# Two DMA queues for loads and stores, and value heads that swap halves as whole rows

## The chip, the cores and the metric

The kernel runs on one core of a Trainium2 chip. The metric is the device time of one execution in microseconds; here four runs gave 533.87 to 536.05 us, with a median of 534.9. The profile is that of one execution, of 533.87 us, in which the core's instructions span 531.9 us.

## The reference

Two layers of the same pair of blocks work on a sequence of 2048 tokens with 512 features, 32 heads of 16. All four blocks read a layer norm of x and add their result to x:

```
for layer in range(2):            # the same weights both times
    x = x + A(layernorm(x))
    x = x + B(layernorm(x))

A: q, k, v = x @ wq, x @ wk, x @ wv, in 4 segments of 512 tokens
   in a segment:  p = softmax(scale * q k^T + mask)    causal, in the segment alone
                  a_dot = p v ; a_mem = phi(q) M / (phi(q) z + 1e-6)
                  o = g * a_mem + (1 - g) * a_dot      g = sigmoid(beta), one per head
   then           M += phi(k)^T v ; z += sum phi(k)
   result         o @ wo

B: q, k, v from x @ wqkv; q, k times w_phi per head
   phi(u) = [softmax(u), softmax(-u)]
   kv = phi(k)^T v and z = sum phi(k), over all tokens
   o = phi(q) kv / (phi(q) z + 1e-6), result o @ wo
```

## The kernel before, in words

x stays in on-chip memory as 16 tiles of 128 tokens (`X`). Each tile is normalised on VectorE (`ln`), with the root taken on GpSimd or ScalarE, and transposed, mostly by a transposing DMA of SyncE (`tr`, L664), so that features stand on partitions. `a_proj` makes keys, queries and values of a segment, `a_att` the attention of a token tile in it, `b_keys` the sums of block B over a segment, and `b_query` its result. `out_proj` transposes the heads' output, multiplies it by the output weights and adds it to x; in the last layer it stores the tile (L1204).

TensorE runs with its array cut in halves of 64 rows: two matmuls, one on partitions 0 to 63 and one on 64 to 127, work side by side (`proj`, `mm`, all recorded at L640). For the products of probabilities and values, half of the heads need their values on the other half of the partitions. So `a_proj` keeps the values of a segment twice: `VT` (pool `pV`), 32 heads with a 17th column of ones, and `VU` (pool `pU`), 16 of the heads with the two partition halves exchanged by two DMAs (L1060, issued at L668). In `VT` heads come in fours, of which the first two are the swapped ones, so each of those DMAs gathers pieces of 2 x 17 values, 68 bytes.

The weights are loaded in `setup`: first four x tiles and the A key and query weights, then (held until tile 3 is normalised) the A value and output weights and x tiles 4 to 7, then (held until tile 7 is normalised) x tiles 8 to 15, the three B weights (`WBraw`) and the B output weights in eight pieces (`WB_o`). All but two small ones are issued by SyncE, at L768. The A value weights are multiplied in place by 1 - g (L855, "gate"). `fold_weights` multiplies w_phi into the B key and query weights: eight transposing DMAs (pX<-pX), eight groups of matmuls (p,pX) and evictions.

The order of all this isn't written out. `Graph` holds every operation with its dependencies, its possible engines and a planned duration. `forward` places operations engine by engine in time by priority, `backward` makes priorities from a placement, and a list of seeds in `STEPS` shifts priorities of some operations at the end; the result is a fixed order for each engine, and waits are put where `emit` finds that they are needed. An operation that may run on one of several engines (an eviction on ScalarE or VectorE, a key mask on VectorE or GpSimd) goes where it can first be placed. The planner keeps one time, `dfree`, at which the loads already issued will have landed. Its durations decide the order alone; the chip decides the times. Where TensorE would stand idle in the plan, it adds matmuls without use (`fill`, L991)[...].

Of the kernel before, what the change touches and what calls it, by code (L numbers as in the profile page):

```python
# [16 lines left out]
H = 32  # L17
# [85 lines left out]
class Graph:  # L103
# [143 lines left out]
    def forward(self, prio, pools, rule):  # L247
# [32 lines left out]
        dfree = 0.0  # L280
# [52 lines left out]
        while len(order) < n + fillers:  # L333
# [25 lines left out]
            for e in TURNS[port_last]:  # L359
# [68 lines left out]
                if o.kb:  # L428
                    dfree = max(dfree, o.end + 1000.0) + o.kb / 0.2
                    o.lat = dfree + 400.0 - o.end  # L430
                order.append(o)
                lt = o.lat if o.lat is not None else LAT[e]
                if o.kind == "d" and e == "sp" and not o.kb:
                    lt = max(lt, dfree - o.end + lt)
# [170 lines left out]
class Kernel:  # L605
# [61 lines left out]
    def dma(self, pairs, n, reads, writes, opens=(), eng="sp", lat=1600.0, label=""):  # L667
        return self.g.op({eng: (650.0 * n, lambda e: [e.dma_start(o, i) for o, i in pairs()])},  # L668
                         reads, writes, opens, kind="d", lat=lat, label=label, ndma=n)
# [91 lines left out]
    def setup(self):  # L761
# [4 lines left out]
        def load(pairs, kb, writes, eng="sp", opens=(), n=1):  # L766
            dur = 780.0 if eng == "pool" else 560.0 if n == 1 else 640.0
            o = self.g.op({eng: (dur * n, lambda e: [e.dma_start(o, i) for o, i in pairs()])}, [], writes, opens, kind="d",  # L768
                          lat=3700.0 if eng == "pool" else 1300.0 + kb / 0.25, label="load", ndma=n, kb=0 if eng == "pool" else kb)
            self.loads.append(o)  # L770
            return o

        def ldx(t0, n):
            load(lambda: [(self.X[:, t0:t0 + n, :], xv[t0 * 128:(t0 + n) * 128, :].rearrange("(t p) d -> p t d", p=128))],
                 128 * n, [R("X", t) for t in range(t0, t0 + n)])

        def ldw(dst, src, res):
            load(lambda: [(dst()[:], src.rearrange("(dt p) o -> p dt o", p=128))], 512, [res])
# [5 lines left out]
        for h in range(2):  # L784
            for k in ("k", "q"):
# [6 lines left out]
        ldw(lambda: self.WA["v"], inp["A_wv"], R("WA", "v"))  # L792
        ldx(4, 4)
        load(lambda: [(self.WA["o"][gi * 64:gi * 64 + 64, 2 * hp:2 * hp + 2, :],
                       inp["A_wo"].rearrange("(hp gi b r) o -> hp gi r b o", hp=2, gi=2, b=2)[hp, gi]) for hp in range(2) for gi in range(2)],
             512, [R("WA", "o")], n=4)
        self.second = len(self.loads)
        ldx(8, 4)
        ldw(lambda: self.WBraw["k"].t, wqkv[:, 512:1024], self.WBraw["k"])
        ldw(lambda: self.WBraw["v"].t, wqkv[:, 1024:1536], self.WBraw["v"])  # L800
        ldx(12, 4)
        ldw(lambda: self.WBraw["q"].t, wqkv[:, 0:512], self.WBraw["q"])
        for g in range(NG):
            load(lambda g=g: [(self.WB["o"][(g % 2) * 64:(g % 2) * 64 + 64, b * 2 + g // 2, :],
                               inp["B_wo"][g * 128 + b * 64:g * 128 + b * 64 + 64, :].rearrange("(h d) o -> d h o", d=16)) for b in range(2)],
                 128, [R("WBo", g)], n=2)
# [47 lines left out]
        for dt in range(4):  # L854
            fn = lambda e, dt=dt: e.tensor_tensor(self.WA["v"][:, dt, :].rearrange("p (h d) -> p h d", h=H),  # L855
                                                  self.WA["v"][:, dt, :].rearrange("p (h d) -> p h d", h=H),
                                                  gt[:, 2, :, None].to_broadcast([128, H, DH]), ALU.mult)
            self.g.op({"dve": (602.0, fn), "pool": (1100.0, fn)}, [R("gt2"), R("WA", "v")], [R("WAv", dt)], label="gate")
# [144 lines left out]
    def a_proj(self, L, s):  # L1003
# [51 lines left out]
        for tp in range(2):  # L1055
            ps = self.T(self.pD, "gen")
            self.vproj(ps, self.WA["v"], [R("WAv", i) for i in range(4)], (2 * tp, 2 * tp + 1), xT, opens=[VT], label="V")
            self.evac(lambda tp=tp: VT.t[:, 2 * tp:2 * tp + 2, :, 0:16], lambda ps=ps: ps.t[:].rearrange("p (t h d) -> p t h d", t=2, h=H),
                      1024, [ps], [VT[2 * tp], VT[2 * tp + 1]], label="Vev")
            self.dma(lambda tp=tp: [(VU.t[64 - 64 * h:128 - 64 * h, 2 * tp:2 * tp + 2].rearrange("p t (u r) c -> p t u (r c)", r=2),  # L1060
                                     VT.t[64 * h:64 * h + 64, 2 * tp:2 * tp + 2].rearrange("p t (u k r) c -> p t u k (r c)", k=2, r=2)[:, :, :, 0])
                                    for h in range(2)], 2, [VT[2 * tp], VT[2 * tp + 1]], [VU[2 * tp], VU[2 * tp + 1]], label="Vx", lat=4000.0)
        if s < 3:
            ps = self.T(self.pD, "gen")

            def phases(ps=ps):
                def item(b, h, g, tt, ph):
                    G = 2 * b + g
                    return (ps.t[:, 512 * b + g * 136:512 * b + g * 136 + 136],
                            st["PhK"][b].t[64 * h:64 * h + 64, g * 512 + tt * 128:g * 512 + tt * 128 + 128],  # L1070
                            VT.t[64 * h:64 * h + 64, tt, 8 * G:8 * G + 8, :], ph == 0 and g == 0 and tt == 0, ph == 1 and g == 1 and tt == 3)
# [41 lines left out]
    def a_att(self, L, s, i):  # L1113
# [9 lines left out]
        for hp in range(2):  # L1123
# [12 lines left out]
            def phases(PV=PV, PTs=PTs, hp=hp, pvv=pvv):  # L1136
# [9 lines left out]
                def item(b, h, gg, hl, j, ph):  # L1146
# [9 lines left out]
                    else:  # L1156
                        val = half(VT.t, h)[:, j, 16 * hp + 8 * gg + 4 * b + hl, :]
# [17 lines left out]
    def out_proj(self, L, t, o, ores, W, wres, store=False, res_pe=False, pe=False, pair=None):  # L1175
# [26 lines left out]
        if store:  # L1202
            self.dma(lambda: [(self.out[0][t * 128:(t + 1) * 128, :], self.X[:, t, :])], 1, [R("X", t)], [], lat=1900.0, label="store")
# [209 lines left out]
def basep(ap):  # L1413
# [17 lines left out]
    830000016, 830000026, 830000031, 830000047, 830000154, 830000166, 830000187, 830000200, 830000233, 830000279,  # L1431
    830000404, 830000410, 830000433, 830000479, 830000580, 830000599, 830000611, 830000784, 830000896, 830000919,
    830001010, 830001382, 830001415, 830001452, 830001504, 830001517, 830002105, 830002116, 830002294, 830002609,
    830002795, 830003279, 830003310, 830003395, 830003781, 830004112, 830004126, 830004203, 830004577, 830004793,
    830004991, 830005011, 830005023, 830005426, 830005440, 830005537, 830005586, 830005719, 830005808, 830006395,
    830006537, 830006565, 830006693, 830006726, 830007056, 830007401, 830007597, 830008013, 830008377, 830008745,
    830008955, 830009116, 830009167, 830009459, 830009499, 830009795, 830010341, 830010604, 830010886, 830010951,
    830011019, 830011698, 830013928, 830014025, 830016905, 830017241, 830017964, 830018111, 830018529, 830018586,
    830021285, 830021587, 830021673, 830023952, 830024198, 830024902, 830026119, 830026354, 830028031, 830029804,
# [53 lines left out]
```

## Time and profile before

| | us |
|---|---|
| median of four runs | 534.9 (533.87 to 536.05) |
| profiled execution | 533.87 |
| its span | 531.9 |
| TensorE busy | 476.4 (90%) |
| ScalarE busy | 449.7 (85%) |
| VectorE busy | 422.1 (79%) |
| GpSimd busy | 139.3 (26%) |
| DMA packets of the main queue | 122288, 32.40 MB, 34.1% of 16 engines' span |
| swaps of values, L668 pU<-pV | 32 issues, 68.0 KB each, 3.0 us to landing at the median |
| transposing DMAs, L664 | 138 issues |
| stores, L668 out_dram<-X | 16 issues, 128.0 KB each, 1.9 us to landing at the median |

An engine is written PE (TensorE), PEld (its weight loads, which overlap the matmuls), DVE (VectorE), ACT (ScalarE), POOL (GpSimd) and SPq (the DMA queue of SyncE). "D<-pQ,pK" means that a tile of pool D is written from tiles of pools pQ and pK; pX holds transposed inputs and raw weights, p is short for the pools p1 and p2. A row of waits gives the microseconds in total, how often, and the longest. Busy shares are averages over stages with different limits, so the stages are looked at one by one. The profile's span begins with the first instruction and ends with the last; the run's time has about 2 us more.

### The profile page before, as it was taken

To read this page: it belongs to the slowest core of one execution; us is meant where nothing else is said; L and a number is where in the kernel's file an instruction comes from. 1 tells how busy PE (TensorE), PEld (TensorE's weight loads), DVE (VectorE), ACT (ScalarE), POOL (GpSimd) and SP (SyncE) were. 2 spreads that over 40 slices of the span, in tenths; PEclk is the share of its full clock that TensorE was granted. 3 is DMA by queue.
4 is the path that set the end of the run, shared out by engine and by line. 5 is a ranking of instruction groups with operands and counts; after the bars stand their busy time and mean duration, and the time that the engine had idled before them with its cause. 6 is when DMAs were issued, how large, how long until landed. Compare 5 with 4: busy or idle time off the path is not lost.

```text
span 531.9 us, 26384 instructions
## 1 busy us (share of the span) xinstructions
PE 476.4 (90%) x12178; PEld 322.2 (61%) x12178; DVE 422.1 (79%) x841; ACT 449.7 (85%) x558; POOL 139.3 (26%) x177
## 2 busy tenths in 40 slices
PE   7988579899999999998999989988999988999887
PEld 3445355566766676765756556565667575655575
DVE  6979278899987888876998868888778986867692
ACT  3889379999889899878798979988989989957894
POOL 5929231440052010000245147521152000100000
PEclk9999799999999999999999989999999999999999
DMA  7176444536224012000147645435112132100265
GB/s 200 45 160 160 99 82 111 64 38 88 43 42 65 14 39 38 14 2 2 25 82 101 102 73 73 92 52 73 42 34 46 49 37 33 23 12 1 52 107 146
DMA packets 122462, 34.10 MB, mean 64 GB/s; under 512 B 109520, under 2 KB 122352, under 8 KB 122352
## 3 DMA queue, kind: packets, MB, share of 16 engines
q1 hardware_dynamic: 122288, 32.40, 34.1%
q8 instruction: 95, 1.56, 1.2%
q14 instruction: 15, 0.12, 0.1%
q0 software_dynamic: 64, 0.02, 0.1%
HBM read 6.32 MB, written 2.10 MB: 16 GB/s over the span
## 4 chain that ended last, share of the span: by engine, by line
PE 48%; ACT 22%; DVE 15%; DMA 8%; issue 3%; SPq 3%; POOL 0%
PE D L640 48%; ACT p L651 14%; DMA p<-p 6%; ACT pP L651 4%; DVE p L1168 2%; SPq L664 2%; DVE stats L913 2%; DVE p L660 1%; DMA pX<-p 1%; DVE pS L1246 1%; ACT p L659 1%; DVE pV L660 1%; DVE pT L1266 1%; DVE p L1341 1%; SPq L1049 1%
## 5 line engine op out<-in xcount | busy, mean ns | idle before, releaser
L651 ACT ACTIVATE p<-D 128x1024 bf16<-128x1024 f32 (+1 forms) x292 | 284.0, 1020 | 44.9 <-PE D L640 42.2
L640 PE MATMUL D<-pQ,pK 64*128 64x256 bf16 (+1 forms) x1344 | 118.3, 261 | 7.2 <-ACT p L651 3.3
L651 ACT ACTIVATE pP<-D 128x768 bf16<-128x768 f32 x128 | 101.8, 820 | 10.9 <-PE D L640 10.1
L921 POOL TENSOR_SCALAR rstd<-mv 128x1 f32<-128x1 f32 x60 | 17.2, 293 | 296.3 <-DVE mv L914 295.4
L1023 POOL TENSOR_SCALAR pK<-p,MK 128x1024 bf16<-128x1024 bf16 x26 | 76.3, 2941 | 34.4 <-DVE p L660 24.4
L640 PEld LDWEIGHTS D<-pQ,pK 64*128 64x128 bf16 x1344 | 56.6, 94 | 43.2 <-ACT p L651 8.8
L640 PE MATMUL D<-pV,p 64*128 64x34 bf16 (+1 forms) x1728 | 67.1, 180 | 1.7 <-issue 1.4
L640 PE MATMUL D<-pU,p 64*128 64x34 bf16 x1536 | 59.8, 176 | 2.2 <-ACT pP L651 0.8
L640 PE MATMUL D<-pU,pP 64*128 64x34 bf16 x1024 | 49.9, 175 | 2.6 <-issue 2.0
L640 PE MATMUL D<-WA_o,p 64*128 64x256 bf16 x520 | 41.4, 280 | 11.9 <-DMA p<-p 10.1
L640 PEld LDWEIGHTS D<-pV,p 64*128 64x128 bf16 x1728 | 50.1, 93 | 2.8 <-issue 2.0
L640 PEld LDWEIGHTS D<-pU,p 64*128 64x128 bf16 x1536 | 46.3, 93 | 7.3 <-ACT pP L651 1.3
L640 PE MATMUL D<-pV,pP 64*128 64x34 bf16 x1024 | 49.9, 175 | 0.3 <-issue 0.3
L1168 DVE TENSOR_TENSOR p<-D,pS 128x256 bf16<-128x256 f32 x112 | 47.1, 421 | 2.8
L913 DVE BATCH_NORM_STATS2 stats<-X 128x6 f32<-128x512 bf16 x64 | 43.4, 686 | 4.0 <-DMA X<-in_A_x_dram 3.2
L1246 DVE TENSOR_REDUCE pS<-p 128x64 f32<-128x1024 bf16 (+1 forms) x36 | 39.0, 1092 | 8.4 <-ACT p L651 8.4
L640 PE MATMUL D<-WB_o,p 64*128 64x256 bf16 x514 | 38.1, 270 | 5.5 <-DMA p<-p 4.1
L1266 DVE TENSOR_TENSOR pT<-D,pT 128x1024 bf16<-128x1024 f32 x32 | 38.8, 1217 | 3.8 <-PE D L640 3.4
L640 PE MATMUL D<-WB_k,pX 64*128 64x512 bf16 (+1 forms) x288 | 33.8, 353 | 6.9 <-issue 4.2
L697 DVE RECIPROCAL pS<-D 128x32 f32<-128x32 f32 (+1 forms) x64 | 20.9, 327 | 20.8 <-PE D L640 20.5
L923 POOL TENSOR_TENSOR rstd<-rstd,mhalf 128x1 f32<-128x1 f32 x60 | 35.5, 597 | 3.5
L1201 DVE TENSOR_TENSOR X<-X,D 128x512 bf16<-128x512 bf16 x32 | 21.8, 681 | 18.3 <-PE D L640 17.9
(124 smaller groups left out, 939.4 us busy)
## 6 DMA issues: line engine op xcount, KB each, us to landing
pQ<-p SPq DMA_DIRECT2D x28, 128.0 KB, 2.2
pU<-pV SPq DMA_DIRECT2D x32, 68.0 KB, 3.0
out_dram<-X SPq DMA_DIRECT2D x16, 128.0 KB, 1.9
X<-in_A_x_dram SPq DMA_DIRECT2D x3, 512.0 KB, 7.1
pX<-in_B_wqkv_dram SPq DMA_DIRECT2D x3, 512.0 KB, 4.9
p<-p SPq DMA_TRANSPOSE x76, 2.7
pX<-p SPq DMA_TRANSPOSE x54, 3.0
X<-in_A_x_dram SPq DMA_DIRECT2D x4, 128.0 KB, 2.5
```

What stands on the lines that cost most here:

```text
L640: ins = e.matmul(out_ap, lhsT, rhs, start=st, stop=sp, tile_position=(basep(lhsT), 0))
L651: return self.g.op({"act": (dur, lambda e: e.activation(out_ap(), in_ap(), func, scale=scale))}, reads, writes, opens, label=label)
L660: "dve": ((340 if fast else n / 0.96 + 65), lambda e: e.tensor_copy(out_ap(), in_ap()))}
L697: return e.reciprocal(o, i)
L913: v(lambda e: e.bn_stats(self.stats[:, t, :], self.X[:, t, :]), 602, [R("X", t)], [R("st", t)], label="bn")
L921: v(lambda e: e.tensor_scalar(rs, self.mv[:, t, 1:2], LN_EPS, None, op0=ALU.add), 240, [R("mv", t)], [R("rstd", t)], eng="pool", label="rstd")
L923: v(lambda e: e.tensor_tensor(rs, rs, self.mhalf[:], ALU.pow), 560, [R("rstd", t), R("mhalf")], [R("rstd", t)], eng="pool", label="rstd")
L1023: return e.tensor_scalar(dst, KT.t[:].rearrange("p (t x c) -> p t x c", x=2, c=64), self.MK[:, 0 if raw else 1, m:m + 1], None, op0=ALU.mult)
L1168: v(lambda e, pvv=pvv, rden=rden, part=part, dst=dst, k=k: e.tensor_tensor(part(dst), pvv()[:, :, k, :, 0:16], rden()[:, :, k, :, None].to ...
L1201: self.v(lambda e: e.tensor_tensor(xt(), xt(), res(), ALU.add), 602, [R("X", t), ps], [R("X", t)], label="res")
L1246: fn = lambda e, sgn=sgn, ev=ev, Z=Z, nz=nz: e.tensor_reduce(Z.t[:, sgn * nz:(sgn + 1) * nz], ev().rearrange("p (h d) -> p h d", d=16), AX ...
L1266: v(lambda e, Vt=Vt, src=src, vt=vt: e.tensor_tensor(vt(Vt, 0, 16), src(), vt(Vt, 16, 17).to_broadcast([128, 2, 2, 2, 16, 8]), ALU.mult), ...
```

## The change

It has three parts, and a new list of seeds.

Loads and stores may be issued by SyncE or by GpSimd: an operation whose engine is "any" has both as candidates, with a planned 560 to 640 ns on one and 780 on the other, and the planner takes whichever can be placed first. That holds for the A value and output weights, x tiles 4 to 15, the B weights and the stores of tiles 0 to 13. The planner's `dfree` becomes one time for each queue.

The A value weights go to a staging tile (`wvraw`, in pool pK) and are multiplied by 1 - g from there into `WA["v"]`, with the heads permuted: the two swapped heads of each four come first, 16 in a row, then the 16 others. The four in-place operations become eight of half the width.

So in `VT` the swapped heads are its first 16, and each swap DMA moves a row of 16 x 17 values, 544 bytes, per partition and tile. The matmuls that read `VT` follow: the memory update takes its eight heads from two places and writes its result in the old order, the probability product counts its heads otherwise. The planner's time for a swap goes from 4000 to 2500 ns.

```diff
-        dfree = 0.0
+        dfree = dict.fromkeys(ENGS, 0.0)
...
-                    dfree = max(dfree, o.end + 1000.0) + o.kb / 0.2
-                    o.lat = dfree + 400.0 - o.end
+                    dfree[e] = max(dfree[e], o.end + (1000.0 if e == "sp" else 2000.0)) + o.kb / 0.2
+                    o.lat = dfree[e] + 400.0 - o.end
...
-    def dma(self, pairs, n, reads, writes, opens=(), eng="sp", lat=1600.0, label=""):
-        return self.g.op({eng: (650.0 * n, lambda e: [e.dma_start(o, i) for o, i in pairs()])},
+    def dma(self, pairs, n, reads, writes, eng="sp", opens=(), lat=1600.0, label=""):
+        return self.g.op({k: ((650.0 if k == "sp" else 780.0) * n, lambda e: [e.dma_start(o, i) for o, i in pairs()]) for k in ((eng,) if eng != "any" else ("sp", "pool"))},
...
         def load(pairs, kb, writes, eng="sp", opens=(), n=1):
-            dur = 780.0 if eng == "pool" else 560.0 if n == 1 else 640.0
-            o = self.g.op({eng: (dur * n, lambda e: [e.dma_start(o, i) for o, i in pairs()])}, [], writes, opens, kind="d",
+            dur = {"pool": 780.0 * n, "sp": (560.0 if n == 1 else 640.0) * n}
+            o = self.g.op({k: (dur[k], lambda e: [e.dma_start(o, i) for o, i in pairs()]) for k in ((eng,) if eng != "any" else dur)}, [], writes, opens, kind="d",
...
         def ldw(dst, src, res):
-            load(lambda: [(dst()[:], src.rearrange("(dt p) o -> p dt o", p=128))], 512, [res])
+            load(lambda: [(dst()[:], src.rearrange("(dt p) o -> p dt o", p=128))], 512, [res], "any")
...
-        ldw(lambda: self.WA["v"], inp["A_wv"], R("WA", "v"))
-        ldx(4, 4)
+        self.wvraw = self.T(self.pK, "raw")
+        wvr = lambda: self.wvraw.t[:].rearrange("p (t o) -> p t o", t=4)
+        ldw(wvr, inp["A_wv"], self.wvraw)
+        ldx(4, 4, "any")
...
         for dt in range(4):
-            fn = lambda e, dt=dt: e.tensor_tensor(self.WA["v"][:, dt, :].rearrange("p (h d) -> p h d", h=H),
-                                                  self.WA["v"][:, dt, :].rearrange("p (h d) -> p h d", h=H),
-                                                  gt[:, 2, :, None].to_broadcast([128, H, DH]), ALU.mult)
-            self.g.op({"dve": (602.0, fn), "pool": (1100.0, fn)}, [R("gt2"), R("WA", "v")], [R("WAv", dt)], label="gate")
+            for w in range(2):
+                def fn(e, dt=dt, w=w):
+                    src = wvr()[:, dt, :].rearrange("p (u w r d) -> p w u r d", w=2, r=2, d=DH)[:, w]
+                    one = gt[:, 2, :].rearrange("p (u w r) -> p w u r", w=2, r=2)[:, w]
+                    dst = self.WA["v"][:, dt, 256 * w:256 * w + 256].rearrange("p (u r d) -> p u r d", r=2, d=DH)
+                    return e.tensor_tensor(dst, src, one[:, :, :, None].to_broadcast([128, 8, 2, DH]), ALU.mult)
+                self.g.op({"dve": (340.0, fn), "pool": (700.0, fn)}, [R("gt2"), self.wvraw], [R("WAv", (dt, w))], label="gate")
...
-            self.dma(lambda tp=tp: [(VU.t[64 - 64 * h:128 - 64 * h, 2 * tp:2 * tp + 2].rearrange("p t (u r) c -> p t u (r c)", r=2),
-                                     VT.t[64 * h:64 * h + 64, 2 * tp:2 * tp + 2].rearrange("p t (u k r) c -> p t u k (r c)", k=2, r=2)[:, :, :, 0])
-                                    for h in range(2)], 2, [VT[2 * tp], VT[2 * tp + 1]], [VU[2 * tp], VU[2 * tp + 1]], label="Vx", lat=4000.0)
+            self.dma(lambda tp=tp: [(VU.t[64 - 64 * h:128 - 64 * h, 2 * tp:2 * tp + 2], VT.t[64 * h:64 * h + 64, 2 * tp:2 * tp + 2, 0:H // 2])
+                                    for h in range(2)], 2, [VT[2 * tp], VT[2 * tp + 1]], [VU[2 * tp], VU[2 * tp + 1]], label="Vx", lat=2500.0)
...
-                            VT.t[64 * h:64 * h + 64, tt, 8 * G:8 * G + 8, :], ph == 0 and g == 0 and tt == 0, ph == 1 and g == 1 and tt == 3)
+                            VT.t[64 * h:64 * h + 64, tt].rearrange("p (w x) c -> p w x c", w=2)[:, :, 4 * G:4 * G + 4, :]
+                            .rearrange("p w (u r) c -> p w u (r c)", u=2), ph == 0 and g == 0 and tt == 0, ph == 1 and g == 1 and tt == 3)
...
-                        val = half(VT.t, h)[:, j, 16 * hp + 8 * gg + 4 * b + hl, :]
+                        val = half(VT.t, h)[:, j, 16 + 8 * hp + 4 * gg + 2 * b + hl - 2, :]
...
-            self.dma(lambda: [(self.out[0][t * 128:(t + 1) * 128, :], self.X[:, t, :])], 1, [R("X", t)], [], lat=1900.0, label="store")
+            self.dma(lambda: [(self.out[0][t * 128:(t + 1) * 128, :], self.X[:, t, :])], 1, [R("X", t)], [], "any" if t < 14 else "sp", lat=2200.0, label="store")
...
-STEPS = (210 seeds, 830000016 to 830141651)
+STEPS = (162 seeds, 910000047 to 910145185)
```

In the new order GpSimd issues the A value weights, the three B weights, one of the two later groups of four x tiles, half of the pieces of `WB_o` and 12 of the 16 stores.

## The prediction

> **What bounds the kernel now.** I read the slices of the span first, then the busy time by stretch, the waits of TensorE, and last the DMA queue of SyncE.
>
> The slices (each digit a tenth, 13.3 us wide):
>
> ```profile
> PE   7988579899999999998999989988999988999887
> ACT  3889379999889899878798979988989989957894
> PEclk9999799999999999999999989999999999999999
> ```
>
> TensorE is at 9 nearly everywhere; it is the bound, with ScalarE close behind. The hole is in slices 5 and 6, where the granted clock dips too. The stretches round it (columns: busy us of TensorE, its weight loads, VectorE, ScalarE, GpSimd; clock; DMA share; GB/s):
>
> ```profile
> 40.00:50.00 10.00, 8.80 (x296) 5.94 (x292) 9.86 (x23) 10.00 (x13) 9.58 (x11) 1.00 0.72 179
> 50.00:60.00 10.00, 5.56 (x118) 4.16 (x112) 5.37 (x14) 6.04 (x7) 6.53 (x8) 0.83 0.47 95
> 60.00:70.00 10.00, 7.01 (x172) 4.95 (x172) 3.97 (x11) 4.47 (x6) 2.58 (x6) 0.83 0.48 93
> 70.00:80.00 10.00, 6.78 (x214) 5.05 (x216) 7.80 (x18) 7.54 (x10) 3.00 (x4) 1.00 0.45 85
> 80.00:90.00 10.00, 9.27 (x230) 6.13 (x228) 8.70 (x17) 9.53 (x11) 1.84 (x2) 1.00 0.46 113
> ```
>
> From 50 to 80 us TensorE is idle 30 - 19.35 = 10.65 us. From 80 to 160 it is idle 5.75 us, 0.72 per 10 us, so 8.5 us are extra. At clock 0.83 the 12.6 us of matmul in 50 to 70 also cost about 2.1 us more. ScalarE is idle 11.95 us there and VectorE 12.86: all starve together, so no other engine eats up what is won here. What TensorE waits for in 50 to 82:
>
> ```profile
> PE D L640 <- DMA p<-p: 4.3, 2, 4.0
> PE D L640 <- DMA pX<-pX: 2.7, 1, 2.7
> PE D L640 <- DMA pX<-p: 1.6, 1, 1.6
> ```
>
> All are transposes issued by SyncE; pX<-pX are the eight that the folding of the B weights needs. Why they are late, in the timeline of SyncE's queue (start, us, line, what):
>
> ```profile
> 34.19 1.13 SPq L768 DMA_DIRECT2D pX<-in_B_wqkv_dram  x2
> 35.36 1.06 SPq L768 DMA_DIRECT2D X<-in_A_x_dram  x2
> 36.46 0.51 SPq L768 DMA_DIRECT2D pX<-in_B_wqkv_dram  x1
> 37.02 5.31 SPq L668 DMA_DIRECT2D pU<-pV  x2
> 42.37 6.59 SPq L768 DMA_DIRECT2D WB_o<-in_B_wo_dram  x6
> ...
> 51.09 3.83 SPq L664 DMA_TRANSPOSE pX<-pX  x2
> ...
> 60.24 1.27 SPq L664 DMA_TRANSPOSE p<-p  x1
> ...
> 70.53 1.28 SPq L664 DMA_TRANSPOSE pX<-pX  x1
> ```
>
> Five loads of 512 KB go out at once, and the small transfers behind them stand still: 5.31 us for two swaps and 6.59 for six loads of 64 KB, where a median issue takes 0.67 and 0.59 us. The queue never rests from 34 to 74 us, so the folding starts at 51.1 and its last transpose leaves at 70.5.
>
> **What the skill says.** "DMA: Bandwidth & Descriptors", Issuing engines are not separate DMA queues: all issuers share 16 DMA engines, and a second one saves issue time alone. Same page, Queues, rings and completion order: each DMA engine goes round-robin between the rows it has work for, packet by packet. So a second issuer brings no bandwidth, but a small transfer no longer stands behind megabytes. The trace of before agrees with the first half: with one queue 37 to 42 us moved 363 GB/s while two swaps took 5.31 us. No run yet shows the round robin. "SBUF — State Buffer", SBUF: two separate sides: DMAs of GpSimd have their descriptors written by software, which VectorE's two-port operations can lock out. Before has only two such DMAs, so this is untested:
>
> ```profile
> L768 POOL DMA_DIRECT2D wphi_st<-in_B_w_phi_dram x1 | 0.8, 797 | 0.0
> L768 POOL DMA_DIRECT2D beta_sb<-in_A_beta_dram x1 | 0.8, 787 | 0.0
> ```
>
> wphi has 512 pieces and beta 128, at nearly the same issue time; a 512 KB load has 512 pieces too, so I take 0.8 us each.
>
> **The change, step by step.** The order of the built kernel shows what its planner made of the freedom. On GpSimd now: the A value weights, the three B weights, one of the two later groups of four x tiles, half of WB_o and 12 of the 16 stores. On SyncE stay two x loads, WA_o, half of WB_o, 4 stores.
>
> (1) *Load stretch, -7.5 us.* From SyncE's queue between 34 and 71.8 us fall four loads (2.7 to 0.5 us), half of WB_o (7.8 with the waits, to 4 x 0.59 = 2.4), and the jam of the two swaps (5.3 to 1.3): 2.2 + 5.4 + 4.0 = 11.6 us, so the last folding transpose is issued at about 60. It may not start too soon: the loads still wait for the normalised tile 7, which now stands in VectorE's order behind some 3.4 us more work (three softplus-type operations 1.5, a mask 0.45, two evictions 1.46): 31.75 + 3.4 = 35.1 instead of 34.2. 2.5 MB at the 363 GB/s measured take 7 us, so the first weight to be folded is in at about 43 and the transposes start there rather than at 51. TensorE's own queue: counting matmul pairs at 0.215 us (512 columns), 0.109 (256) and 0.026 (34), all from spacings in the trace, before has 39.9 us of work ahead of the first fold and 51.2 ahead of the first B projection, reached at 55.6 and 77.9: 11.3 us of work in 22.3. At the pace of the rest (386 us of work in 451, 1.17) it would take 13.2; 9.1 are lost, in keeping with the 10.6 above. I take 9.5. In the new order the folds stand at 35.7 to 47.8 us of work; at a lag of 13 us (15.7 less the 2.7 waited at the first fold) plus 2 the last is reached at about 63, just when its transpose, issued at 60, lands (3.6 us at the median). That is tight, so I leave 2 us lost. Bounds: 0 to -10.6.
>
> (2) *Stores, -1 us.* From 497 us SyncE's queue is full, with nine stores (some 0.58 us each, 5.2 in all) between the last transposes, and TensorE waits 3.8 us for p<-p after 495. GpSimd is idle there (0.00 busy from 480). But the last transposes of the chain left 0.04 us after VectorE had their operand, so little of it was the queue's. Bounds 0 to -3.
>
> (3) *Swap in 544-byte rows, -0.5 us.* A swap falls from 64 x 16 = 1024 pieces of 68 B to 128. Its issue stays near 0.65 us. The two in 425 to 429 took all DMA engines for 2 x (0.56 + 0.45) = 2.0 us, so 32 take some 32 us of the 181 (34.1% of the span) that the queue's packets fill. No wait of TensorE on pU shows, so the gain is only that transposes beside them land sooner. Bounds 0 to -2.
>
> (4) *Gates, +0.3 us.* Four operations of 0.67 us (one 1.52) become eight of half the size, at 0.35 to 0.42 (a 128x256 product with PSUM takes 0.42): 3.0 to 3.4 against 2.7. VectorE is 9.97 of 10 us busy in 20 to 30, so it counts. Bounds 0 to +1.
>
> (5) *Issues on GpSimd, +0.5 us.* Nine before 45 us, 9 x 0.79 = 7.1 us, fall into its idle time (29.3 to 39.0) and 3 us beyond; behind them wait the key masks of segment 1 and the roots for tiles 8 to 11. The 12 stores have nothing behind them. Bounds 0 to +2, and rival B.
>
> (6) *Free.* The memory-update matmuls read 2 x 68 columns in two strips, still 136; the values sit elsewhere in V, with no operation added. If strips cost 10%, 96 pairs at 0.06 us make 0.6.
>
> (7) *All orders after 80 us are new.* Work is the same: about 439 us of queued matmuls in both, 561 ScalarE instructions against 560, 166 fillers against 156. I see no sign, so 0, with +-4.
>
> Sum: -7.5 - 1 - 0.5 + 0.3 + 0.5 = -8.2 on the profiled execution's 533.9, 525.7 (span 523.7). The median of the runs is 1.0 above that execution, so 526.7.
>
> **Rivals.** *A, the stretch is hidden or refilled (530 to 536).* The weights come, but TensorE then stands before the next late thing (layer norm, transposes of the B input; pX<-p is already 1.6 us of the waits). For it: slices 5 to 6 hold several kinds of wait. Against: all engines starve together, and 8 transposes leave 11 us earlier. Half of (1): -4 instead of -8.2, 531; nothing: 534.9.
> *B, slower (537 to 546): the software queue delivers the weights late.* Three loads of 512 KB, starved or issued at 2 to 3 us each, push folding behind 51. That is the point from which it decides: weights in at 51 cancel (1), at 60 they cost 9 us: 534.9 + 8 = 543. For it: no large load on GpSimd is in the trace, and VectorE is full there. Against: 0.79 us whatever the piece count; wphi landed in 4.9 us.
> *C, more (516 to 523):* all of (1), -10.6, with stores and swaps at half their bounds, -2.5: 521.8.
>
> **Chances.** Main case (523 to 530) 0.48, C 0.15, A 0.14 with a gain and 0.07 without a difference, B 0.16. A difference under 0.3% (533.3 to 536.5) is about what this kernel's runs can't tell from none. So faster 0.77, same 0.07, slower 0.16. From 520 to 536.5, 0.8 are held: B goes, and the low end of C. The main case alone: 523 to 530.
>
> **What would show it.** Right: pX<-pX transposes start near 43 and end near 60; two swaps at about 1.3 us; TensorE idle in 50 to 80 near 4.5 us; clock 1.0; the first B projection near 70. Wrong: weights landing after 50, GpSimd issues above 1.5 us, or the hole gone from there and open elsewhere after 80.

## The result, and the profile after

The changed kernel takes 538.9 us at the median (533.6 to 544.0, 43 runs); the kernel before, run beside it, takes 535.0. The ratio is 1.0055, 95% interval 1.0039 to 1.0072: slower by some 3 us, where 526.7 was predicted. A ratio here compares the means of the executions within 1.5% of the fastest of the same kernel, so it isn't the quotient of two medians. The profiled execution of the changed kernel is one of its longer ones (543.2 us, span 541.5, granted clock 0.977 where the one of before had 0.99), so its lines say where time is lost and not how much.

The slices of the changed kernel, 13.5 us wide:

```profile
PE   7785978899999989999889879899999989899985
ACT  3853989799999989858979769899789989957973
PEclk9987999899999999999999989999999999999998
```

The hole has not closed, it has moved forward: TensorE is at 7, 8 and 5 in slices 2 to 4, and slices 5 and 6, where the hole of before was, have 9 and 7. The busy time by stretch (the columns are those of the prediction's table):

```profile
20.00:30.00 10.00, 6.88 (x46) 2.06 (x44) 7.88 (x12) 7.23 (x13) 10.00 (x5) 0.83 0.00 1
30.00:40.00 10.00, 8.43 (x171) 4.85 (x168) 8.14 (x18) 6.83 (x10) 3.98 (x6) 0.92 0.37 70
40.00:50.00 10.00, 5.59 (x88) 4.15 (x84) 4.16 (x6) 5.15 (x6) 3.26 (x6) 0.84 1.02 245
50.00:60.00 10.00, 7.96 (x152) 4.16 (x152) 3.56 (x9) 5.31 (x6) 3.17 (x2) 0.73 0.61 128
60.00:70.00 10.00, 8.77 (x286) 6.89 (x288) 9.64 (x26) 9.80 (x13) 9.60 (x16) 1.00 0.46 99
70.00:80.00 10.00, 7.49 (x218) 5.32 (x214) 6.36 (x13) 8.10 (x11) 6.76 (x10) 1.00 0.44 84
```

From 50 to 80 us TensorE is busy 24.2 us, 4.9 more than before; from 20 to 50 it is busy 20.9, where before had 8.39 + 9.47 + 8.80 = 26.7. So 5.8 us are lost ahead of the place where 4.9 are won. In the stretch from 40 to 50 us the DMA engines are full (1.02).

What waited there, in the waits of TensorE and of VectorE:

```profile
PE D L640 <- DMA pX<-p: 6.1, 1, 6.1
PE D L640 <- DVE WA_v L862: 2.9, 1, 2.9
...
DVE WA_v L862 <- DMA pK<-in_A_wv_dram: 2.8, 1, 2.8
```

Neither of the first two waits was in the kernel before (its 1.6 us for pX<-p came at 77.9 us, ahead of the first B projection). One is for a transposed x tile, the other for the gated A value weights, which VectorE could not start because they had not landed. The queues tell why. GpSimd's queue in the timeline of the changed kernel, then SyncE's:

```profile
8.97 0.78 POOL L768 DMA_DIRECT2D pK<-in_A_wv_dram  x1 [1.06 <-DVE p L939]
...
38.18 2.31 POOL L768 DMA_DIRECT2D pX<-in_B_wqkv_dram  x3 [5.93 <-DVE p L939]
40.48 0.75 POOL L768 DMA_DIRECT2D X<-in_A_x_dram  x1
41.22 2.04 POOL L768 DMA_DIRECT2D WB_o<-in_B_wo_dram  x4
```

```profile
34.36 7.63 SPq L664 DMA_TRANSPOSE pX<-p  x4
42.04 0.78 SPq L768 DMA_DIRECT2D X<-in_A_x_dram  x1
42.87 3.36 SPq L768 DMA_DIRECT2D WB_o<-in_B_wo_dram  x4
47.19 1.35 SPq L668 DMA_DIRECT2D pU<-pV  x2
48.58 3.29 SPq L664 DMA_TRANSPOSE pX<-pX  x2
...
73.10 1.27 SPq L664 DMA_TRANSPOSE pX<-pX  x1
```

The four transposes are those of x tiles 4 to 7. Before, they left SyncE ahead of the loads, from 28.46 on, and the loads behind them went out from 34.19 on. Now GpSimd issues 1.5 MB of B weights at 38.18, while the last transpose leaves SyncE only at 39.14. The record of those four in the kernel before, then in the changed kernel:

```profile
L664 SPq DMA_TRANSPOSE pX<-p x4: 1188/1264/1312, 28.5 to 32.9; - x4
...
DMA to landing us min/median/max: 2.4/2.5/2.5
```

```profile
L664 SPq DMA_TRANSPOSE pX<-p x4: 1190/1278/2850, 34.4 to 39.1; - x4
...
  PE D L640: 6.1, 1
...
DMA to landing us min/median/max: 2.5/4.2/12.5
```

One took 12.5 us to land. The chain that ended last runs straight through it: "39.14 12.50 DMA pX<-p", with TensorE's next matmuls at 51.69.

Some things did go as meant. The two swaps that took 5.31 us take 1.35, the main queue carries 88928 packets where it had 122288, and GpSimd issues a load in 0.77 us.

### The profile page after: what moved, and what is told of

It is laid out like the page before. It is cut to its first block, busy times and chain, and to the rows that moved or that the text cites. A ratio compares the mean times of both kernels' runs of the same rounds, so it can differ in the third digit from the quotient of the medians.

```text
span 541.5 us, 26326 instructions
## 1 busy us (share of the span) xinstructions
PE 483.9 (89%) x12146; PEld 323.3 (60%) x12146; DVE 420.7 (78%) x843; ACT 447.8 (83%) x559; POOL 153.1 (28%) x199
## 3 DMA queue, kind: packets, MB, share of 16 engines
q1 hardware_dynamic: 88928, 27.94, 26.8%
## 4 chain that ended last, share of the span: by engine, by line
PE 50%; ACT 18%; DMA 14%; DVE 14%; issue 2%; SPq 1%; POOL 0%; POOLq 0%; DVEq 0%
PE D L640 49%; ACT p L651 13%; DMA p<-p 7%; DMA pX<-p 4%; ACT pP L651 3%; DVE p L660 2%; DVE stats L918 2%; DMA pK<-in_A_wv_dram 1%; DVE p L1173 1%; DVE pS L1251 1%; DVE p L1346 1%; ACT p L659 1%; DVE WA_v L862 1%; DVE pS L697 1%; DMA pX<-pX 1%
## 5 line engine op out<-in xcount | busy, mean ns | idle before, releaser
L640 PE MATMUL D<-pQ,pK 64*128 64x256 bf16 (+1 forms) x1354 | 119.7, 264 | 11.1 <-ACT p L651 6.3
L1028 POOL TENSOR_SCALAR pK<-p,MK 128x1024 bf16<-128x1024 bf16 x27 | 78.6, 2919 | 79.1 <-DVE p L660 47.1
L640 PE MATMUL D<-WA_o,p 64*128 64x256 bf16 x512 | 39.2, 272 | 5.7 <-DMA p<-p 4.4
L640 PE MATMUL D<-WB_o,p 64*128 64x256 bf16 x516 | 39.6, 277 | 4.4 <-DMA p<-p 3.9
L660 DVE CAST p<-D 128x1024 bf16<-128x1024 f32 (+2 forms) x29 | 32.2, 1109 | 12.2 <-PE D L640 12.1
L640 PE MATMUL D<-WA_v,pX 64*128 64x512 bf16 x256 | 34.3, 391 | 3.0 <-DVE WA_v L862 2.9
L640 PE MATMUL D<-pX,WA_k 64*128 64x512 bf16 x224 | 31.0, 398 | 6.6 <-DMA pX<-p 6.1
```

The costliest lines, as they stand in the source:

```text
L640: ins = e.matmul(out_ap, lhsT, rhs, start=st, stop=sp, tile_position=(basep(lhsT), 0))
L660: "dve": ((340 if fast else n / 0.96 + 65), lambda e: e.tensor_copy(out_ap(), in_ap()))}
L1028: return e.tensor_scalar(dst, KT.t[:].rearrange("p (t x c) -> p t x c", x=2, c=64), self.MK[:, 0 if raw else 1, m:m + 1], None, op0=ALU.mult)
```

## The experiments

Every kernel was timed against runs of the kernel before on the same chip, whose medians were 534.8 to 538.0 us. Kernels named `a_` have the order of the changed kernel, those named `b_` the order of the kernel before; within a letter the instructions of TensorE, VectorE and ScalarE stand in the same order (gates apart), and only what is named differs. In the `b_` kernels with rows the gates are four operations of two halves each, and the value weights are staged in another place.

| kernel | what it has | ratio to before, 95% interval |
|---|---|---|
| the change | new order, rows, queues | 1.0055 (1.0039 to 1.0072) |
| a_wv | value weights back on SyncE | 0.999 (0.9963 to 1.0016) |
| a_hold | late loads of GpSimd held | 0.9937 (0.9894 to 0.998) |
| a_wv_hold; again | both | 0.992 (0.9886 to 0.9953); 0.999 (0.9954 to 1.0025) |
| a_loads_sp | all loads on SyncE | 0.9981 (0.9952 to 1.001) |
| b_rows | rows alone | 0.9886 (0.9826 to 0.9946) |
| b_pool_again | queues alone | 0.9967 (0.9944 to 0.9991) |
| b_rows_pool | rows and queues | 0.9925 (0.9898 to 0.9952) |
| b_rows_stores | rows, stores on GpSimd | 0.9855 (0.982 to 0.9891) |
| b_rows_hold | rows, held loads | 0.9885 (0.986 to 0.9911) |
| b_rows_hold_stores; again | rows, held loads, stores | 0.979 (0.9746 to 0.9834); 0.9893 (0.9809 to 0.9977) |
| b_rows_four | rows, four issues to a swap | 1.0052 (1.0027 to 1.0077) |
| b_rows_small2 | four issues, pieces of 68 bytes | 1.0146 (1.0102 to 1.0191) |

Two kernels were measured twice, on different chips, and moved by 0.7 and 1.0%. So kernels of one set of runs are compared more freely than kernels of different sets, where a difference under 1% is a hint at most. The sets are: a_wv, a_hold, a_loads_sp, b_rows; a_wv_hold, b_rows_pool, b_rows_hold, b_rows_stores; b_rows_hold_stores, b_rows_small2; b_rows_four and the two repeats; and b_pool_again by itself. Medians of all runs give a smaller gain than the ratio for a_hold (0.9974) and for b_rows_pool (0.9955).

**Are the late transfers the loss?** In the changed kernel's order the two late transfers were mended one at a time. All such edits move single operations in the finished order, before the waits are put in; `loads[10]` are the A value weights, `loads[11]` x tiles 4 to 7. For a_wv:

```diff
+        od = self.g.order
+
+        def to(o, eng, after=None, deps=()):
+            o.ch = {**o.ch, eng: next(iter(o.ch.values()))}
+            o.eng = eng
+            o.deps.update(deps)
+            if after is not None:
+                od.remove(o)
+                od.insert(od.index(after) + 1, o)
+
+        to(self.loads[10], "sp", self.loads[11])
```

> The changed kernel, every engine in its order, with one load moved: the A value weights are issued by SyncE again, between x tiles 4 to 7 and the A output weights. My theory (two queues let loads overtake what is waited for): the weights land about 4.8 us after their issue instead of 7.5, the gates and all behind them start some 2.5 us sooner, and the time falls by 1.5 to 3 us, to about 0.995 of the changed kernel. Rival (the new order as a whole is the loss, wherever loads are issued): less than 1 us.

Measured: 537.5 us. Against the change that is 0.65% or 3.5 us, but from two sets of runs, so the size is a hint. The weights land in 4.7 us where GpSimd's issue took 7.5, and the four transposes leave from 30.81 instead of 34.36. The other wait stays and even grows, since the loads follow the same tiles forward: TensorE waits 7.9 us for pX<-p, and the slowest transpose takes 12.7 us to land. So the two waits are separate.

For a_hold, GpSimd's late loads depend on the four transposes as well:

```diff
+        xt = [o for o in od if o.label == "xnT" and o.eng == "sp"][:4]
+        last = xt[3]
+        for k in (15, 17, 14, 13, 21, 18):
...
+            to(self.loads[k], "pool", last, xt)
+            last = self.loads[k]
```

> The changed kernel in its order, with the loads that GpSimd issues at 38 to 43 us (three B weights, x tiles, half of the B output weights) waiting until the four transposes of x tiles 4 to 7 have landed. Theory: those transposes land in about 2.5 us each instead of up to 12.5, TensorE's wait of 6.1 us for them goes, the weights come some 4 us later, and the time falls by 2 to 5 us. Rival (folding is what counts, and is only made later): no gain or a loss of up to 3 us.

Measured: 536.3 us, ratio 0.9937. The four transposes:

```profile
L664 SPq DMA_TRANSPOSE pX<-p x4: 1188/1280/2023, 32.5 to 36.8; - x4
...
DMA to landing us min/median/max: 2.5/2.9/3.8
```

3.8 us at most, and TensorE's wait for them is gone. The loads start 2.5 us later than in the change, at 40.71, and the kernel is 1.2% faster nevertheless (1.0% by the medians). With both edits (a_wv_hold):

> The changed kernel with both mends: value weights issued by SyncE, and the late loads on GpSimd waiting until the four transposes of x tiles 4-7 have landed. Theory (two separate losses that add): ratio to before 0.986 to 0.991, near the rows alone. Rival (the two hide behind one another, or the new order has a loss of its own): 0.993 to 0.998, as with one mend.

The first time 531.8 us, ratio 0.992, just above the range of the theory and 1.35% below the change. The second time 0.999, just above the range of the rival. Both are below the change, by 0.65 to 1.35%; that is what the two late transfers together cost it, as far as these runs tell. That the two losses add, as the theory had it, is not shown: a_hold alone has 0.9937. In the traces both mends work: TensorE waits for neither transfer, and the slowest of the four transposes lands in 4.1 us.

The other cure is to put all loads back on SyncE, behind the four transposes (a_loads_sp). It is the edit of a_wv and this:

```diff
+        for k in (15, 17, 14, 13, 21, 18):
+            to(self.loads[k], "sp", last)
+            last = self.loads[k]
```

> The changed kernel in its order, with every load of weights and x issued by SyncE again, the late ones right behind the four transposes of tiles 4 to 7, as before the change; stores stay on both. Theory: the early loss goes, as both competing transfers are gone, and the time comes to that of before or below, 4 to 7 us under the changed kernel; the small loads and swaps behind the late loads jam again for about 10 us in SyncE's queue. Rival (the order is the loss): within 1.5 us of the changed kernel, above before.

Measured: 537.2 us, ratio 0.9981. The wait is gone here too (slowest landing 3.9 us), but the loads fill SyncE's queue again, and TensorE waits 6.0 us for an eviction of VectorE (p L660). That is 0.75% better than the change, a hint at most between two sets, and worse than a_hold, in the same set, by 0.4% with overlapping intervals.

**What is each part worth without the new order?** First the rows alone: before's order and queues, with the gates, swaps and matmuls of the change's diff, and a staging place that needs no tile of pool pK:

```diff
-        ldw(lambda: self.WA["v"], inp["A_wv"], R("WA", "v"))
+        ldw(lambda: self.WB["v"], inp["A_wv"], R("WA", "v"))
```

> The kernel before, every engine in its old order, with the value part of the change alone: permuted value weights (the four gate operations become eight halves, from a staging place), swaps in rows of 544 bytes, all queues as before. Theory: a gain of 0.5 us, at most 2, since no wait for the swaps shows; main-queue packets fall from 122288 to about 93600. Rival (the gates on the crowded VectorE cost more than the swaps save): a loss of up to 1 us.

Measured: 530.7 us, ratio 0.9886, about 6 us faster than before. SyncE's queue:

```profile
36.77 1.92 SPq L668 DMA_DIRECT2D pU<-pV  x2
38.73 4.75 SPq L768 DMA_DIRECT2D WB_o<-in_B_wo_dram  x6
...
44.85 3.20 SPq L664 DMA_TRANSPOSE pX<-pX  x2
...
65.44 1.27 SPq L664 DMA_TRANSPOSE pX<-pX  x1
```

All loads are still ahead of the swaps in this queue, and yet the two swaps take 1.92 us instead of 5.31 and the six loads behind them 4.75 instead of 6.59. The folding's transposes start at 44.85 instead of 51.09 and end 5.1 us earlier. The first B projection starts at 72.5, where before had 77.9, so most of the gain is made by then (the two profiled executions are 6.6 us apart). So the jam came not from the loads alone but from small pieces among loads. The pieces also fill the DMA engines for longer: with the same 32.40 MB, the main queue's packets take 32.6% of this span, 171 us, where they took 181.

Then the queues alone (b_pool_again): GpSimd issues the same loads and twelve stores as in the change, with 68-byte pieces:

```diff
+        for k in (10, 15, 17, 14, 13, 21, 18):
+            to(self.loads[k], "pool")
+        for o in [o for o in od if o.label == "store"][:12]:
+            to(o, "pool")
```

> The order and the 68-byte pieces of the kernel before, with the later loads and the first twelve stores issued by GpSimd: the queues alone. Theory A, the one on record in step 1 of the prediction (SyncE's queue is relieved and the fold's transposes go out earlier): faster by 4 to 8 us, ratio 0.985 to 0.993. Theory B (the loads on the second queue overtake the transposes of x tiles 4-7, and what they lose eats the relief): 0.997 to 1.006, with a wait for a transposed x tile of 4 us or more between 30 and 45 us.

Measured: 533.4 us, ratio 0.9967: between the two theories, at the edge of B. The whole is worth 0.3%, and what theory B names is in the trace: one of the transposes lands after 8.3 us, and TensorE stands 5.6 us for it. The relief that theory A counts on did not come. SyncE's queue in this kernel:

```profile
33.68 0.67 SPq L768 DMA_DIRECT2D X<-in_A_x_dram  x1
36.24 4.97 SPq L668 DMA_DIRECT2D pU<-pV  x2
41.26 6.18 SPq L768 DMA_DIRECT2D WB_o<-in_B_wo_dram  x4
...
50.73 3.59 SPq L664 DMA_TRANSPOSE pX<-pX  x2
...
69.67 1.27 SPq L664 DMA_TRANSPOSE pX<-pX  x1
```

Four of the five big loads have left this queue, and still the two swaps take 4.97 us, where they took 5.31, and the last of the folding's transposes leaves at 69.67, where it left at 70.53. Part of that may be time lost in the wait before: the queue stands empty from 47.4 to 49.5. Rows and queues together, with both edits (b_rows_pool):

> The order of the kernel before, the value part in 544-byte rows, and the later loads (A value weights, three B weights, x tiles, WB_o) and the first twelve stores issued by GpSimd: all of the change except its newly planned order. Theory (the loads on the second queue overtake the transposes and the value weights land late, which is the loss): the gain of the rows alone is lost again, 3 to 8 us above b_rows, ratio to before 0.993 to 1.005; a transpose of x tiles 4-7 lands in over 8 us and the value weights in over 7. Rival (the new order is the loss): stays at 0.985 to 0.991 like b_rows, though the same transfers are late in the trace.

Measured: 534.2 us, ratio 0.9925. The transposes in this kernel, and who waited for them:

```profile
L664 SPq DMA_TRANSPOSE pX<-p x4: 1188/1266/1297, 28.1 to 32.5; - x4
...
  PE D L640: 5.4, 1
...
DMA to landing us min/median/max: 2.4/3.5/8.2
```

A third of the gain of the rows is gone by the ratios, and more by the medians, though the intervals of b_rows_pool and b_rows overlap; the traces agree, with the first B projection at 77.2 in place of 72.5. Here too the loads leave GpSimd (at 31.70) before the last transpose leaves SyncE (32.5). The two swaps take 1.26 us, where the same queues with small pieces had 4.97. One half of the theory failed: the value weights landed in 5.8 us, not in over 7, and nothing waited for them. With the edit of a_hold in its place, and value weights and stores on SyncE (b_rows_hold):

> The order of the kernel before, the value part in 544-byte rows, the late loads (three B weights, x tiles, WB_o) on GpSimd but waiting until the four transposes of x tiles 4-7 have landed; value weights and stores on SyncE. Theory (a second queue helps when its loads don't race the transposes): fold transposes go out 3 to 6 us earlier than in b_rows, ratio to before 0.980 to 0.989. Rival (with the rows the SyncE queue is no longer what bounds this stretch): same as b_rows, 0.986 to 0.992.

Measured: 530.2 us, ratio 0.9885, with the four transposes at 2.4/2.5/2.5 again: held loads cost nothing, but bring no gain over the rows alone, as the rival said. In the same set of runs b_rows_pool is 0.4% slower, with intervals that just overlap. The rows and the two lines for the stores (b_rows_stores):

> The order of the kernel before, the value part in 544-byte rows, and the first twelve stores on GpSimd. Theory (the stores' queue is worth next to nothing): within 0.3% of b_rows, ratio to before 0.985 to 0.992. Rival (stores held behind GpSimd's own work cost buffers, or free SyncE for its transposes): 0.3 to 1% off b_rows to either side.

Measured: 528.1 us, ratio 0.9855. In the same set of runs that is 0.3% below b_rows_hold, with overlapping intervals; a gain of 1 us or so is possible and not shown. Held loads and stores together (b_rows_hold_stores):

> The order of the kernel before, the value part in 544-byte rows, the late loads on GpSimd but waiting for the four transposes of x tiles 4-7, and the first twelve stores on GpSimd; value weights on SyncE. Theory (loads that don't race and stores off SyncE each take work from its queue, and add): ratio to before 0.980 to 0.986, below each alone. Rival (once the swaps are rows, SyncE's queue no longer bounds anything): 0.985 to 0.990, no better than the rows alone.

Measured: 527.2 us, ratio 0.979, below the range of the theory. The second run (below) gave 0.9893, which is where the rival had it; so whether holds and stores add to the rows stays open.

**Pieces or issues?** To give the swaps their 68-byte pieces back without anything else, the target of a swap got a gap of 2 bytes after each 34 values. This version writes such a transfer tile by tile, in four issues instead of two (b_rows_small2; the lines are those that differ from b_rows, without the matmuls' reading of the gapped tile and four small constants that share a tile to make room for it):

```diff
-        self.pU = pool("pU", 2, [128, 4, H // 2, 17], BF16, {}, ("VU",))
+        self.pU = pool("pU", 2, [128, 4, H // 4, 35], BF16, {}, ("VU",))
...
-            self.dma(lambda tp=tp: [(VU.t[64 - 64 * h:128 - 64 * h, 2 * tp:2 * tp + 2], VT.t[64 * h:64 * h + 64, 2 * tp:2 * tp + 2, 0:H // 2])
-                                    for h in range(2)], 2,
+            self.dma(lambda tp=tp: [(VU.t[64 - 64 * h:128 - 64 * h, t, :, 0:34],
+                                      VT.t[64 * h:64 * h + 64, t, 0:H // 2].rearrange("p (u r) c -> p u (r c)", r=2))
+                                    for h in range(2) for t in (2 * tp, 2 * tp + 1)], 4,
```

> The kernel with the rows alone (b_rows), in the same order, but each swap moves its bytes in pieces of 68 bytes again, 1024 to a pair of tiles and half as before the change, into a target with gaps of 2 bytes and in four issues where there were two; weights, gates and matmuls stay those of the rows. Theory (the gain of the rows is the small pieces that clog SyncE's queue behind the loads): the gain goes, ratio to before 0.996 to 1.004, and the swap issued near 37 us takes 4 us or more. Rival (the gain comes from the gates, the staging or chance of the order): stays at 0.985 to 0.992.

Measured: 545.6 us, ratio 1.0146. The gain goes, and more than the gain. So the number of issues had to be tried by itself (b_rows_four, also against b_rows):

```diff
-            self.dma(lambda tp=tp: [(VU.t[64 - 64 * h:128 - 64 * h, 2 * tp:2 * tp + 2], VT.t[64 * h:64 * h + 64, 2 * tp:2 * tp + 2, 0:H // 2])
-                                    for h in range(2)], 2,
+            self.dma(lambda tp=tp: [(VU.t[64 - 64 * h:128 - 64 * h, t], VT.t[64 * h:64 * h + 64, t, 0:H // 2])
+                                    for h in range(2) for t in (2 * tp, 2 * tp + 1)], 4,
```

> The kernel with the rows alone (b_rows), in the same order, with each swap in four issues of 64 rows where it had two of 128: the control for b_rows_small2, which had four issues too. Theory (the small pieces did it, not the number of issues): within 0.5% of b_rows, ratio to before 0.985 to 0.993. Rival (the two issues more of each swap hold up SyncE as much as the pieces do): 1.000 to 1.015, as b_rows_small2.

Measured: 539.2 us, ratio 1.0052: the rival was right for a large part. SyncE's queue of b_rows_four, then of b_rows_small2:

```profile
24.54 5.45 SPq L668 DMA_DIRECT2D pU<-pV  x8
30.03 5.22 SPq L664 DMA_TRANSPOSE pX<-p  x4
...
39.29 4.17 SPq L668 DMA_DIRECT2D pU<-pV  x4
43.49 3.81 SPq L768 DMA_DIRECT2D WB_o<-in_B_wo_dram  x6
```

```profile
24.52 5.71 SPq L668 DMA_DIRECT2D pU<-pV  x8
30.28 5.23 SPq L664 DMA_TRANSPOSE pX<-p  x4
...
39.69 6.30 SPq L668 DMA_DIRECT2D pU<-pV  x4
46.04 6.24 SPq L766 DMA_DIRECT2D WB_o<-in_B_wo_dram  x6
```

Eight issues instead of four hold the transposes of tiles 4 to 7 back by 1.9 us (30.03 against 28.13), and TensorE is busy 6.8 us from 30 to 40 in place of 9.6. By the first B projection b_rows_four is 4.9 us behind b_rows (77.4 against 72.5), and at the end of the profiled executions 11.9 us (that of b_rows is its fastest); so about half of what the issues cost is lost later, and where is open.

At equal issues, the four swaps and six loads take 12.5 us with small pieces instead of 8.0, the first B projection comes at 80.2 instead of 77.4, and the kernel is slower by another 0.9%, with separate intervals though on different chips. Without loads in front the pieces hardly show in the queue: the eight swaps at 24.5 take 5.71 us against 5.45. The matmuls that read the gapped tile are not the reason, with a mean of 176 ns in both kernels. So the pieces account for the shorter jam, and most of the rows' gain is made behind it; that they are all of the 1.1% is not shown, since 0.9% between two chips is a hint. More issues on SyncE cost more than the pieces do: 1.7% for 32 of them, again between two chips.

**Has the new order a loss of its own?** The changed kernel with both mends differs from b_rows_hold_stores in the planned order, and in the form and the staging place of the gates. They were run side by side once more.

> The kernel of b_rows_hold_stores once more, beside the next one on the same chip. If the newly planned order has a loss of its own, this one is 3 to 8 us below mended_again (ratio to before 0.976 to 0.984); if the order costs nothing, the two are within 1.5 us of one another.

> The kernel of a_wv_hold once more: the changed kernel's order with both mends, for the direct comparison with best_again, from which it differs in the planned order alone. Loss of the order: ratio to before 0.989 to 0.995. No loss of the order: as best_again.

Measured: 534.0 us and 0.9893 against 535.0 us and 0.999. By these ratios the order costs 1.0%, and by the first runs (0.979 and 0.992, from different chips) 1.3%; but by the medians it costs 0.2%, and the intervals overlap. A loss of the order itself is likely, somewhere from 1 to 7 us, and its size stays open. It would lie behind the load stretch: in single executions the first B projection starts at 74.3 in the mended change against 75.3 in the first pair, and at 76.6 against 76.4 in the second.

## Why the prediction was wrong

**The sum is met by luck, and by a kernel that was not the one measured.** Rows alone are worth -6.1 us, give or take 3, and queues alone -1.8 (0.0114 and 0.0033 of 537); their sum, -7.9, is almost the -8.2 of the prediction. But the prediction gave the rows -0.5 and the queues nearly all the rest, so the terms were the wrong way round. Together they give -4.0, and with the order that the change brings +3. The prediction added parts that share one queue, left out what they do to a third party, and gave the order no sign.

**Step (1), the load stretch (-7.5), is where it failed.** It says that the jam of the swaps falls from 5.3 to 1.3 us when the loads leave, and the last folding transpose goes out at about 60. With the queues alone the swaps take 4.97 us and that transpose goes at 69.67 (b_pool_again). Its last link is that the folding starts earlier, and no term of it asks what stands beside the loads when they leave. The queue of before did two things: it made the folding wait, which I saw, and it kept 2.5 MB behind the transposes of x tiles 4 to 7, which I did not. On a second queue the loads pass them, and one transpose takes 12.5 us instead of 2.5. The prediction had the Trainium skill for this: "DMA: Bandwidth & Descriptors", Queues, rings and completion order, has each DMA engine take turns between queue rows by packets. From that I drew that a small transfer no longer stands behind megabytes. For these transposes the runs say otherwise: 12.5 and 8.2 us beside loads of the other queue, 3.8 and 2.5 with those loads held. Whether the turns are uneven or a transpose needs many of them, no run tells; the measurement decides that the conclusion was wrong.

The times of the step follow. First folding transpose: predicted 43, measured 48.6. Last: predicted 60, measured 73.1, later than before. First B projection: predicted 70, measured 83.4, where before had 77.9. The loads' start was predicted at 35.1, the end of the normalisation of tile 7; that ended at 38.2.

**Step (1) also took the rows' gain for the queue's.** The 4.0 us for the jam of the swaps were put down to the loads' leaving. b_rows has the loads still there and 1.92. **Step (3)**, the rows, was then sized at -0.5, "no wait of TensorE on pU shows": true, and the wrong place to look. A swap that nobody waits for still stands in a queue in front of transposes that TensorE waits for. Measured: -6.1 us. The same page of the skill, Why small descriptors are slow (HBM only), says that transfers within on-chip memory don't suffer from small pieces. Here they do: the same bytes in as many issues take 12.5 us of the queue against 8.0 behind loads, and fill the DMA engines for 181 us against 171 in the whole kernel. The measurement decides.

**Step (5), issues on GpSimd (+0.5), had the right price for the wrong thing.** An issue takes 0.77 us, as taken. But no term has a later landing of the A value weights, and it was 7.5 us against 4.8. They are the first of the moved loads, and their eight gates stand in VectorE's fixed order in front of the statistics of tiles 5 to 7: VectorE waits 2.8 us, TensorE 2.9. a_wv prices this at some 3.5 us, between two sets of runs. In the old order the same load from GpSimd landed in 5.8 us and nobody waited (b_rows_pool). The prediction moved this load without asking who stands behind the first gate.

**Step (7), the new order (0, +-4)**, is +1.3% or 7 us between b_rows_pool and the change, from different sets of runs. Most of it shows by the first B projection, which starts at 83.4 in the (longer) profiled execution of the change and at 77.2 in that of b_rows_pool. The race of loads and transposes is in both, but the new order makes it worse: a landing of 12.5 us where b_rows_pool has 8.2, and the wait for the value weights besides. With the two mends 0.65 to 1.35% of the change's time comes back. A possible reason stands in the diff: `dfree` was one time for all transfers, so the planner counted a small transfer of SyncE as landed only after all loads issued until then; with one time for each queue it sees neither that loads of the other queue can delay it nor by how much. That this is why the order came out so was read from the code; a new plan with one `dfree` was not run.

**The small ones.** (2) stores, -1: b_rows_stores is in keeping with it and doesn't show it; in the change itself TensorE's wait for p<-p after 495 us is 3.9, where it was 3.8. (4) gates, +0.3: the eight take 4.7 us in the change, against 3.4 for four, so +1.3 there, but 3.3 in b_rows. (6) no sign of a cost: the memory-update matmuls take 7.7 us before and 7.8 in the change.

**The rivals.** Rival B was right in kind, transfers late through the software queue, and its range of 537 to 546 held the result. Its place was wrong: it let the B weights decide, at a landing after 51. They were issued at 38.2 and took 7.6 us at the median, with 8.3 at most, so all three were in by about 48, and B's own condition did not come about. What was late were the tiles and weights that the prediction did not follow. So its range holding the result was luck in part. A chance of 0.16 for it was too low in view of a new order and a queue that no run had yet shown under load.

## What to carry to other kernels

When loads leave a queue, list what they stood behind as well as what stood behind them: a queue is also a schedule, and a second one needs an explicit wait in place of the order that it gives up. Cut the number of pieces of a transfer in a crowded queue even where nobody waits for the transfer itself, and don't pay for it with more issues. Put parts on the chip one at a time before summing them: -6.1 and -1.8 were -4.0 together. The best version that these runs point to is the old order with rows, held loads and stores on GpSimd (0.979 and 0.989 of before), but the rows alone give 0.9886 with the smallest edit, and that the rest adds to them is not shown.

## What the hardware showed that was not expected

A hole in TensorE's work cost more than its length here. In stretches of 5 us of the changed kernel round the wait of 6.1 us (columns as above, for 5 us each):

```profile
40.00:45.00 5.00, 5.00 (x84) 3.96 (x82) 0.46 (x1) 3.56 (x5) 3.26 (x6) 0.82 0.98 280
45.00:50.00 5.00, 0.59 (x8) 0.20 (x4) 3.70 (x6) 1.60 (x2) 0.00 (x0) 0.87 1.06 210
50.00:55.00 5.00, 3.31 (x18) 1.27 (x20) 1.45 (x3) 0.96 (x1) 0.00 (x0) 0.50 1.16 246
55.00:60.00 5.00, 4.64 (x136) 2.89 (x132) 2.11 (x6) 4.36 (x6) 3.17 (x2) 0.95 0.05 11
```

TensorE is busy 0.59 us from 45 to 50, and the granted clock is 0.50 in the next 5 us, so that 3.31 us of matmul time there did half the work: by estimate 1.7 us more on top of the hole. The Trainium skill describes this in "TensorE: Matmul & The Clock Gate", HAM oscillation — how this bites in real kernels: a wait for data makes the clock fall, and the next work starts cold. The trace agrees, and also in other kernels: 0.50 from 45 to 50 us in a_wv, behind 5 us with no matmul at all.

One transpose was five times slower than its neighbour: 2.5 us at the least and 12.5 at the most among four issued within 5 us. And DMA issues on SyncE, 0.6 to 0.7 us each, were dear: 32 more of them in the whole kernel, b_rows_four against b_rows, took it from 0.9886 to 1.0052 of before, the two measured on different chips.
